# Clustered attention with token mixing: a twelve-slot plan for the two row halves of TensorE, small products in the maxima's PSUM tiles, and six weight conversions moved from the first half of the kernel to the second

## The chip, the cores and the metric

One core of one Trainium2 chip runs the whole kernel. The metric is device time in microseconds (us). Engines are named as in the profile: PE (TensorE matmul), PEld (its weight loads), DVE (VectorE), ACT (ScalarE), POOL (GpSimd), and SP, which issues nearly all DMAs; all but PEld take their instructions strictly in the order of their queue.

## The reference

```python
# attention: q, k, v are (4, 8, 768, 64), centroids (8, 16, 64)
q_assign = argmax(einsum('bhsd,hcd->bhsc', q_n, c_n)); k_assign likewise      # normalised rows
scores = where(q_assign[..., :, None] == k_assign[..., None, :], q @ k.T / sqrt(64), -1e9)
attn = exp(scores - max(scores)); attn = attn / (sum(attn) + 1e-9); x = attn @ v
# token mixing: x is (4, 768, 512)
theta = x @ w_theta
y = w_tok_r @ (x * cos(theta)) + w_tok_i @ (x * sin(theta))
u = x + y
return u + maximum(u @ w_ch, 0)
```

The weights arrive as 64-bit floats and are turned into 32-bit ones on the chip: one chunk is a DMA, an Abs on ACT, four integer and clamp operations on DVE (`to_f32`), a copy on ACT (the high part) and a subtraction on POOL (the low part).

## The kernel before

**Attention.** Two heads form a pair; there are 16 pairs. A pair has two halves `a` of 384 queries, and a half has six units, one for each block of 128 keys: 12 units a pair, 192 in all, numbered `u`. The main loop does two units in a pass, so a pair takes six passes. They are called pass 0, 2, 4, 6, 8 and 10 here, by `u` modulo 12.

In the PE the two heads of a pair use different halves of the 128 rows (`j` = 0: rows 0 to 63, `j` = 1: rows 64 to 127), so that two matmuls run beside each other; such a place in time is a *slot*. A pass has:

- the scores of two units, `sc`: four matmuls for each unit and head (`hk·hq`, `hk·lq`, `lk·hq`, and the mask and shift rows `mk·mq`), 8 slots; each unit and head fills one PSUM bank, of which there are three, and ACT reads it as an exponential into `at` (`exps`);
- the running maximum of a unit that is `LEAD` = 10 ahead, `m`: four matmuls for each head, 4 slots; each head fills one *maximum's tile* of two banks (tag `m`, two buffers), which DVE reduces to `nm` (`max_of`, the instruction at L396);
- the weighted sums `av` of the two units before (`weighted`): eight instructions of 32-bit floats;
- POOL adds the exponentials (`add_exps`), DVE adds two of those sums at `ADDS` (`acc` from `acc` and `acc`, L452).

**The small pieces.** `todo` holds pieces of work with a unit number at which they are issued (`at_unit`, `stages`); `pieces(x)` issues all up to x. For the pair after the next, `assign` finds the clusters: `lg` (centroid products, PE), `lt` (its transpose, PE; DVE then takes the maximum `mxl`, the equality and its product with the cluster numbers `eq`, and the maximum `rr`), `rt` (PE), a DMA round trip into `clq` and `clk`, and the mask rows `mq` and `mk`. `shift_row` transposes the row maxima (`mt`), `sums` adds over keys (`sm`, then a DMA round trip with a reciprocal on DVE), `normalise` scales `xt` on POOL. In the kernel before, `lg`, `mt`, `sm` use one of the three score banks, `lt` a maximum's tile, and all follow the weighted sums. After them, a pass ends with a further group of four slots.

Within attention `in_order` fixes the order of every engine as the code writes it. Instructions of the token mixing are ordered by the scheduler.

**The conversions.** `early_weights` converts 16 chunks during attention, one every 12 units: `w_theta` (4), the first three row blocks of `w_tok_r` and `w_tok_i` (6), and the last three of each (6), which are written back to DRAM in 32 bits (`w_d`). In the mixing, `late` loads these six (`kept`), splits them with one ACT copy and one DVE subtraction each, and converts `w_ch` (4 chunks).

**Token mixing.** 24 steps (4 batches × 6 blocks `t`): `theta` two steps ahead of `mix`; after six steps `channel` adds y and multiplies by `w_ch`. Step (0, t) of the first batch needs `w_r[t]` and `w_i[t]`.

Of the kernel before, what the change touches and what calls it, by code (L numbers as in the profile page):

```python
# [9 lines left out]
F32 = mybir.dt.float32  # L10
# [15 lines left out]
SUMS = (4, 6, 8, 9, 10)  # L26
# [3 lines left out]
EARLY = 3  # L30
NAT = 6
# [10 lines left out]
def kernel(  # L42
# [62 lines left out]
    ncl = cpool.tile([P, 1], F32, name="ncl")  # L105
    nc.vector.tensor_scalar_mul(ncl, mcl, -1.0)
# [43 lines left out]
    def split_w(hi, lo, src, cols, new, eng, most, kept=None):  # L150

        def chunk(sl):
            w = yield from to_f32(src[:, sl], sl.stop - sl.start, new)
            yield
            if kept is not None:
                nc.sync.dma_start(out=kept[:, sl], in_=w)
                return
            nc.scalar.copy(out=hi[:, sl], in_=w)
            eng.tensor_tensor(out=lo[:, sl], in0=w, in1=hi[:, sl].bitcast(F32), op=ALU.subtract)
# [15 lines left out]
    w_d = {(t, x): dram.tile([P, S], F32, name=f"wd{t}{x}") for t in range(EARLY, NT) for x in "ri"}  # L175
# [6 lines left out]
    ps = actx.enter_context(tc.tile_pool(name="ps", bufs=8 - 2 * N_M - N_AV, space=PSUM))  # L182
# [16 lines left out]
    def bank(name):  # L199
        return ps.tile([P, 512], F32, tag="bank", name=name)  # L200
# [47 lines left out]
    def assign(pi):  # L248
# [11 lines left out]
        lg = bank(f"lg{pi}")[:, 0:HS]  # L260
# [11 lines left out]
        for t in range(HS // P):  # L272
# [8 lines left out]
            out=eq, in0=ltv, in1=mx.unsqueeze(2).broadcast_to([P, NG, C]), op=ALU.is_equal)  # L281
        yield

        nc.vector.tensor_tensor(out=eq, in0=eq, in1=wb, op=ALU.mult)
# [29 lines left out]
        else:  # L314
            rt = bank(f"rt{pi}")[0:NG, 0:P]
# [23 lines left out]
        nc.vector.tensor_scalar(  # L339
            out=st[pi]["mk"], in0=cl["k"], scalar1=mcl, scalar2=mbi, op0=ALU.not_equal, op1=ALU.mult)  # L340
# [59 lines left out]
    def shift_row(pi, a):  # L400

        s = st[pi]
        mt = bank(f"mt{pi}{a}")
# [17 lines left out]
    def score_products(u, j, banks=None):  # L421
# [5 lines left out]
        sc = banks[:, j] if banks else ps.tile([P, 512], F32, tag="bank", name=f"sc{u}_{j}")  # L427
# [4 lines left out]

    def exps(u, j):

        pi, a, i = split_u(u)
        s = st[pi]
        last_exp[0] = nc.scalar.activation(out=s["at", a, i][:, j], in_=s["sc", j], func=AF.Exp, scale=SCALE)  # L437

    def add_exps(u):
# [6 lines left out]
        if y > 0:  # L446
            prev = s["at", a, i - 1] if y == 1 else s["acc", a, x]
            last_acc[0] = nc.gpsimd.tensor_tensor(out=s["acc", a, x], in0=prev, in1=at, op=ALU.add)  # L448

# [85 lines left out]
    def early_weights():  # L535
# [5 lines left out]
        for t in range(EARLY, NT):  # L541
            for x, src in (("r", wrT), ("i", wiT)):
                yield from split_w(
                    None, None, src[t * P:(t + 1) * P], S, raw_pair, nc.gpsimd, CKE, kept=w_d[t, x])
# [107 lines left out]
    A_UNITS = (-9, -4, -2, -1, 2, 2, 3, 6, 7, 7.9)  # L652
# [8 lines left out]
    A_THIRD = (-9, -1, 0, 1, 4, 4, 5, 7, 8, 9)  # L661
    W_EVERY = 12
# [17 lines left out]
    part_lo(0, "k", nc.gpsimd)  # L680
    load_v(0)
    in_order(start)
    for pi in range(NPAIR):
# [4 lines left out]
        for a in range(2):  # L688
            at_unit(u + a * NT - LEAD + NT, shift_row, pi, a)
# [317 lines left out]
```

## Time and profile before

| what | value |
|---|---|
| time, median of 3 runs | 791.12 us (791.0 to 792.93) |
| the profiled execution: its time, its span | 792.87 us, 791.1 us |
| mean granted PE clock | 0.991 |
| attention (up to the last `sm`) | to about 455.7 us |
| PE busy, DVE busy, POOL busy, ACT busy | 98%, 72%, 62%, 49% of the span |
| DMA | 73.43 MB |

The first half of the profile's 40 slices shows PE, DVE and POOL at 8 or 9 tenths at once, the second half only PE. A busy PE in this profile says that some matmul is recorded as running, not that they follow each other as closely as they can; gaps between the starts of matmuls are read from the timeline.

### The profile page before, as it was taken

To read this page: it belongs to the slowest core of one execution; us is meant where nothing else is said; L and a number is where in the kernel's file an instruction comes from. 1 tells how busy PE (TensorE), PEld (TensorE's weight loads), DVE (VectorE), ACT (ScalarE), POOL (GpSimd) and SP (SyncE) were. 2 spreads that over 40 slices of the span, in tenths; PEclk is the share of its full clock that TensorE was granted. 3 is DMA by queue.
4 is the path that set the end of the run, shared out by engine and by line. 5 is a ranking of instruction groups with operands and counts; after the bars stand their busy time and mean duration, and the time that the engine had idled before them with its cause. 6 is when DMAs were issued, how large, how long until landed. Compare 5 with 4: busy or idle time off the path is not lost.

```text
span 791.1 us, 14306 instructions
## 1 busy us (share of the span) xinstructions
PE 774.3 (98%) x5538; PEld 572.9 (72%) x5538; DVE 572.6 (72%) x688; ACT 386.5 (49%) x777; POOL 488.3 (62%) x284
## 2 busy tenths in 40 slices
PE   6999999999999999999999799999999999999998
PEld 4656665666656565656665488899889988899998
DVE  5789999999999999999989659954445433634322
ACT  3366666767676676767556436341334123403310
POOL 3388789999999999888988432561215122332131
PEclk9899999999999999999999999999999999999999
DMA  3132324332433244324343467115011411030001
GB/s 120 61 98 72 93 95 151 93 123 91 151 104 125 81 149 151 119 84 164 112 161 109 101 182 206 24 31 173 15 27 28 160 27 27 14 94 15 1 21 61
DMA packets 81583, 73.43 MB, mean 93 GB/s; under 512 B 59588, under 2 KB 65324, under 8 KB 81132
## 3 DMA queue, kind: packets, MB, share of 16 engines
q1 hardware_dynamic: 81228, 72.10, 30.5%
q8 instruction: 43, 0.70, 0.4%
q10 hardware_dynamic: 288, 0.43, 0.1%
q14 instruction: 24, 0.20, 0.1%
HBM read 57.08 MB, written 15.32 MB: 92 GB/s over the span
## 4 chain that ended last, share of the span: by engine, by line
PE 91%; DVE 5%; DMA 2%; issue 1%; SPq 1%; ACT 1%; DVEq 0%
PE y L876 26%; PE sc L374 24%; PE av L509 15%; PE tp L608 8%; PE cy L899 5%; PE m L374 4%; PE cp L899 3%; PE sm L476 2%; PE lg L263 2%; PE y L899 1%; DVE acc L452 1%; PE lt L275 1%; DVE nm L396 1%; PE mt L404 1%; DVE xl L583 1%
## 5 line engine op out<-in xcount | busy, mean ns | idle before, releaser
L437 ACT ACTIVATE at<-sc 128x384 f32<-128x384 f32 x384 | 173.6, 493 | 96.0 <-PE m L374 50.5
L396 DVE TENSOR_REDUCE nm<-m 128x1 f32<-128x768 f32 x192 | 179.6, 945 | 21.4 <-PE m L374 18.3
L448 POOL TENSOR_TENSOR acc<-at,at 128x768 f32<-128x768 f32 x64 | 129.9, 2030 | 36.0 <-ACT at L437 36.0
L374 PE MATMUL m<-hk,hq 64*128 64x384 f32 x384 | 147.1, 387 | 0.9 <-DVE nm L396 0.8
L509 PE MATMUL av<-at,vt 128*64 128x384 f32 x768 | 145.7, 499 | 1.4 <-ACT at L437 1.2
L830 POOL TENSOR_TENSOR zlc<-ab,zhc 128x512 fp32r<-128x512 f32 x24 | 32.1, 1336 | 173.2 <-ACT zhc L828 173.2
L448 POOL TENSOR_TENSOR acc<-acc,at 128x768 f32<-128x768 f32 x64 | 132.4, 2068 | 10.1 <-ACT at L437 8.0
L374 PE MATMUL m<-mk,mq 64*128 64x384 f32 x384 | 127.7, 336 | 0.8 <-DVE mk L303 0.8
L374 PE MATMUL sc<-hq,hk 64*128 64x384 f32 x384 | 116.6, 388 | 0.5 <-ACT at L437 0.5
L374 PEld LDWEIGHTS sc<-hq,hk 64*128 64x128 f32 x384 | 55.8, 184 | 62.7 <-issue 27.9
L374 PE MATMUL sc<-mq,mk 64*128 64x384 f32 x384 | 97.6, 335 | 0.0
L374 PE MATMUL sc<-hq,lk 64*128 64x384 f32 x384 | 97.3, 334 | 0.0
L374 PE MATMUL sc<-lq,hk 64*128 64x384 f32 x384 | 97.3, 334 | 0.0
L509 PEld LDWEIGHTS av<-at,vt 128*64 128x64 f32 x768 | 46.7, 136 | 60.5 <-issue 53.6
L374 PEld LDWEIGHTS m<-hk,hq 64*128 64x128 f32 x384 | 70.7, 185 | 3.4 <-DVE nm L396 2.8
L374 PEld LDWEIGHTS m<-mk,mq 64*128 64x128 f32 x384 | 71.6, 188 | 1.1 <-ACT hq L356 1.1
L613 DVE TENSOR_SCALAR kk<-tp 128x512 int32<-128x512 f32 x24 | 16.4, 683 | 77.2 <-PE tp L608 77.2
L452 DVE TENSOR_TENSOR acc<-acc,acc 128x768 f32<-128x768 f32 x30 | 70.6, 2354 | 0.0
L581 ACT CAST xh<-xT 128x512 fp32r<-128x512 f32 x23 | 14.3, 622 | 99.7 <-PE tp L608 99.7
L890 POOL TENSOR_TENSOR ul<-xT,uh 128x384 fp32r<-128x384 f32 (+1 forms) x36 | 33.5, 957 | 35.4 <-ACT uh L889 34.9
L374 PEld LDWEIGHTS sc<-lq,hk 64*128 64x128 f32 x384 | 54.9, 186 | 0.0
L374 PEld LDWEIGHTS sc<-mq,mk 64*128 64x128 f32 x384 | 54.7, 184 | 0.0
(160 smaller groups left out, 1710.3 us busy)
## 6 DMA issues: line engine op xcount, KB each, us to landing
rawq<-in_qT_dram SPq DMA_DIRECT2D x16, 384.0 KB
vt<-in_v_dram SPq DMA_DIRECT2D x16, 384.0 KB
rb<-sd SPq DMA_DIRECT2D x32, 192.0 KB
xT_d<-xt SPq DMA_DIRECT2D x16, 384.0 KB
xb<-xT_d SPq DMA_DIRECT2D x96, 64.0 KB
rawk<-in_kT_dram SPq DMA_DIRECT2D x15, 384.0 KB
w<-in_wrT_dram SPq DMA_DIRECT2D x6, 768.0 KB
w<-in_wiT_dram SPq DMA_DIRECT2D x6, 768.0 KB
```

The source lines that it names most:

```text
L374: nc.tensor.matmul(out, lhsT=stat[r, cols], rhs=mov[r, over], start=start, stop=stop)
L396: nc.vector.tensor_reduce(out=s["nm", a][:, j, i // 2:i // 2 + 1], in_=s["m", j][:, :, 0:HS], op=ALU.max, axis=AX.XY, negate=True)
L437: last_exp[0] = nc.scalar.activation(out=s["at", a, i][:, j], in_=s["sc", j], func=AF.Exp, scale=SCALE)
L448: last_acc[0] = nc.gpsimd.tensor_tensor(out=s["acc", a, x], in0=prev, in1=at, op=ALU.add)
L452: nc.vector.tensor_tensor(out=s["acc", a, 0], in0=s["acc", a, 0], in1=s["acc", a, 1], op=ALU.add)
L509: nc.tensor.matmul(s["av"][64 * j:64 * j + 64], lhsT=s["vt"][:, i, j, :], rhs=s["at", a, i][:, j], start=(i == 0), stop=(i == NT - 1))
L608: nc.tensor.matmul(tp, lhsT=xx[:, c, :], rhs=w_th[c][k], start=(n == 0), stop=(n == 3 * NCT - 1))
L613: nc.vector.tensor_scalar_mul(kk, tp, INV_2PI)
L830: nc.gpsimd.tensor_tensor(out=zl, in0=tr, in1=zh.bitcast(F32), op=ALU.subtract)
L876: nc.tensor.matmul(y_at(b, d, c0, c1), lhsT=zz[:, d * P:(d + 1) * P], rhs=ww[:, c0:c1], start=first and lead, stop=last, skip_group_check= ...
L890: nc.gpsimd.tensor_tensor(out=ul[:, d, :], in0=x, in1=uh[:, d, :].bitcast(F32), op=ALU.subtract)
L899: nc.tensor.matmul(cp, lhsT=w_c[d][k][:, e * P:(e + 1) * P], rhs=uu[:, d, :], start=(n == 0), stop=(n == 3 * NCT - 1), skip_group_check=True)
```

## The change

1. **A pass in twelve slots.** While maxima are still to be made, `two_units(u, v)` replaces the three groups. Each row half has its own list: rows `j` = 0 hold the last slot of the scores (u-1, 0), then m(v, 0) in slots 1 to 4, sc(u, 0) in 5 to 8, and the first three slots of sc(u+1, 0) in 9 to 11, whose fourth is carried into the next pass; rows `j` = 1 hold sc(u, 1) in 0 to 3, m(v, 1) in 4 to 7, sc(u+1, 1) in 8 to 11. The exponentials follow after slots 0, 3, 8 and 11, `max_of` after 4 and 7. The pieces of `pieces(u - 0.5)` and the weighted sums come after slot 11.
2. **Banks by a plan.** `bank` picks the score bank that a count of slots (`free_at`) says is free first.
3. **Small pieces.** `lg`, `rt`, `mt` and `sm` now take a maximum's tile, and by their new unit numbers (`SUMS`, `A_UNITS`, `shift_row` half a unit earlier) all stand in front of the weighted sums, after the twelve slots.
4. **Masks.** `mk` is made by one ACT pass (Abs with a scale and bias for each partition), `mq` by one DVE pass; before, `mq` took two ACT passes and `mk` one on DVE. The constants are made by `mask_constants`. The equality of `lt` is written in place in PSUM, and its product with the cluster numbers reads it from there.
5. **Conversions.** The six chunks that went through DRAM are no longer converted in attention. The remaining nine after the first start at units 0, 12, 36, 48, 72, 84, 108, 120, 144. `late` converts the six from the 64-bit input as 12 chunks of 384 columns, `LATE` says after which.
6. An explicit wait of `exps(u, 0)` on the adds and exponentials of unit u-5.

```diff
-SUMS = (4, 6, 8, 9, 10)
+SUMS = (3.5, 6, 8, 9, 10)
+LATE = (1, 3, 6, 8)
...
+    def bank(name, until=None):
+        x = min(range(NB), key=lambda i: (free_at[i], i))
+        free_at[x] = until if until is not None else clock[0] + AV_SLOTS
+        return ps.tile([P, 512], F32, tag=f"bank{x}", name=name)
...
-        lg = bank(f"lg{pi}")[:, 0:HS]
+        lg = (m_tile(f"lg{pi}")[:, 0] if pi > 2 else bank(f"lg{pi}"))[:, 0:HS]
...
         nc.vector.tensor_tensor(
-            out=eq, in0=ltv, in1=mx.unsqueeze(2).broadcast_to([P, NG, C]), op=ALU.is_equal)
-        yield
-
-        nc.vector.tensor_tensor(out=eq, in0=eq, in1=wb, op=ALU.mult)
+            out=ltv, in0=ltv, in1=mx.unsqueeze(2).broadcast_to([P, NG, C]), op=ALU.is_equal)
+        nc.vector.tensor_tensor(out=eq, in0=ltv, in1=wb, op=ALU.mult)
+        yield
...
-            nc.scalar.activation(out=mq, in_=cl["q"], func=AF.Abs, bias=ncl)
-            yield
-            nc.scalar.activation(out=mq, in_=mq, func=AF.Relu, scale=-1.0, bias=1.0)
+        nc.scalar.activation(out=st[pi]["mk"], in_=cl["k"], func=AF.Abs, scale=kscale, bias=kbias)
         yield
         nc.vector.tensor_scalar(
-            out=st[pi]["mk"], in0=cl["k"], scalar1=mcl, scalar2=mbi, op0=ALU.not_equal, op1=ALU.mult)
+            out=st[pi]["mq"], in0=cl["q"], scalar1=mcl, scalar2=-1.0, op0=ALU.is_equal, op1=ALU.mult)
...
-        mt = bank(f"mt{pi}{a}")
+        mt = m_tile(f"mt{pi}{a}")[:, 0] if pi + a > 0 else bank(f"mt{pi}{a}")
...
+        v = u + 1 - NAT
+        for x in (adds[v], exp_of[v, 0], exp_of[v, 1]) if j == 0 and v in adds else ():
+            tc.add_manual_dep(last_exp[0].ins, x.ins.name, ...)
...
+        begin = {
+            0: (scores, u, 1, 0, 4), 1: (maxima, 0, 1), 4: (maxima, 1, 4), 5: (scores, u, 0, 5, 9),
+            8: (scores, u + 1, 1, 8, 12), 9: (scores, u + 1, 0, 9, SLOTS + AV_SLOTS + 1)}
+        end = {
+            0: first, 3: [(exps, u, 1), (weighted_out, u - 3)], 4: [(max_of, v, 0)], 7: [(max_of, v, 1)],
+            8: [(exps, u, 0), (add_exps, u)], 11: [(exps, u + 1, 1)]}
+        for k in range(SLOTS):
+            ...
+            interleave(*([rows[j, k]] for j in range(2) if (j, k) in rows))
+            for fn, *a in end.get(k, ()):
+                fn(*a)
...
-        sm = bank(f"sm{pi}") if pi < NPAIR - 1 else ...
+        sm = m_tile(f"sm{pi}")[:, 0] if pi < NPAIR - 1 else ...
...
-    A_UNITS = (-9, -4, -2, -1, 2, 2, 3, 6, 7, 7.9)
+    A_UNITS = (-9, -2.5, -0.5, 0, 1.5, 2, 3, 7, 7.9)
-    W_EVERY = 12
...
-            at_unit(u + a * NT - LEAD + NT, shift_row, pi, a)
+            at_unit(u + a * NT - LEAD + NT - (0.5 if pi + a > 0 else 0), shift_row, pi, a)
...
-        stages(W_FIRST if x == 0 else [W_EVERY * (x - 1) + k for k in W_UNITS], gen)
+        stages(W_FIRST if x == 0 else [NU * (3 * (x - 1) // 2) + k for k in W_UNITS], gen)
...
-        if 0 <= u < NUT:
+        if 0 <= u and ahead < NUT:
+            two_units(u, ahead)
+        elif 0 <= u < NUT:
+            finish(u - 1)
             both(score_products, u, exps)
...
     def late():
-        for t in range(EARLY, NT):
-            for w, x in ((w_r, "r"), (w_i, "i")):
-                hi, lo = w[t]
-                kept = u_tile("kept").rearrange("p c s -> p (c s)").bitcast(F32)[:, 0:S]
-                nc.sync.dma_start(out=kept, in_=w_d[t, x])
-                nc.scalar.copy(out=hi, in_=kept)
-                nc.vector.tensor_tensor(out=lo, in0=kept, in1=f(hi), op=ALU.subtract)
...
+        rows = [(w[t], src, S, t) for t in range(EARLY, NT) for w, src in ((w_r, wrT), (w_i, wiT))]
+        rows += [(w_c[c], w_ch, DM, c) for c in range(NCT)]
+        for x, (hi_lo_, src, cols, r) in enumerate(rows):
+            for gen in split_w(*hi_lo_, src[r * P:(r + 1) * P], cols, wt_pair, nc.gpsimd, CK):
+                run(gen)
+            if x in LATE:
+                yield
```

**Two places in the order of the engines.** Names carry the unit (`m156_0`: unit 156, head 0; the number behind it counts tiles). Unit 144 is pass 0 of pair 12, unit 146 pass 2; the maxima made there are those of units 154 and 156.

DVE from pass 0 to pass 2, before:

```order
L396 TENSOR_REDUCE nm150_4569<-m152_1_4638 128x1
L278 TENSOR_REDUCE mxl14_4660<-lt14_4656 128x24
L280 TENSOR_TENSOR eq14_4662<-lt14_4656,mxl14_4660 128x384
L396 TENSOR_REDUCE nm150_4569<-m152_0_4665 128x1
L284 TENSOR_TENSOR eq14_4662<-eq14_4662,wc_74 128x384
L286 TENSOR_REDUCE rr14_4678<-eq14_4662 128x24
L396 TENSOR_REDUCE nm150_4569<-m154_1_4695 128x1
L396 TENSOR_REDUCE nm150_4569<-m154_0_4713 128x1
L452 TENSOR_TENSOR acc139_4547<-acc139_4547,acc142_4634 128x768
L396 TENSOR_REDUCE nm156_4745<-m156_1_4746 128x1
L137 TENSOR_SCALAR w32_4605<-w32_4605 128x768
L396 TENSOR_REDUCE nm156_4745<-m156_0_4777 128x1
```

DVE at the same place, now:

```order
L403 TENSOR_REDUCE nm150_4516<-m154_0_4631 128x1
L403 TENSOR_REDUCE nm150_4516<-m154_1_4639 128x1
L291 TENSOR_REDUCE mxl14_4668<-lt14_4664 128x24
L293 TENSOR_TENSOR lt14_4664<-lt14_4664,mxl14_4668 128x384
L295 TENSOR_TENSOR eq14_4670<-lt14_4664,wc_74 128x384
L299 TENSOR_REDUCE rr14_4678<-eq14_4670 128x24
L471 TENSOR_TENSOR acc139_4514<-acc139_4514,acc142_4601 128x768
L403 TENSOR_REDUCE nm156_4689<-m156_0_4690 128x1
L403 TENSOR_REDUCE nm156_4689<-m156_1_4699 128x1
```

The four steps behind `lt` and the add of `acc` now stand in one run between the second maximum of pass 0 and the first of pass 2; before, a maximum stood between them at two places.

PE at the end of pass 2's slots, before (`m156_1` is the maximum's tile filled last; `mt121` holds the transposes of the row maxima and of `rr`):

```order
L374 MATMUL sc147_0_4744<-mq_0_165,mk_0_166 128x384
L374 MATMUL m156_1_4746<-mk_1_148,mq_1_147 128x384
L509 MATMUL av144_4758<-at144_4680,vt12_4550 64x384 x2
L509 MATMUL av144_4758<-at145_4693,vt12_4550 64x384 x2
L404 MATMUL mt121_4763<-identf_64,nm150_4569 6x128
L312 MATMUL mt121_4763<-identf_64,rr14_4678 24x128
L374 MATMUL sc147_1_4776<-hq_0_161,hk_0_163 128x384
L374 MATMUL m156_0_4777<-hk_1_145,hq_1_143 128x384
```

PE at the same place, now:

```order
L381 MATMUL sc147_0_4717<-hq_0_155,lk_0_158 128x384
L381 MATMUL sc147_1_4712<-mq_0_159,mk_0_160 128x384
L411 MATMUL mt121_4725<-identf_64,nm150_4516 6x128
L325 MATMUL mt121_4725<-identf_64,rr14_4678 24x128
L567 MATMUL av144_4735<-at144_4625,vt12_4506 64x384 x2
L567 MATMUL av144_4735<-at145_4651,vt12_4506 64x384 x2
L381 MATMUL sc147_0_4717<-mq_0_159,mk_0_160 128x384
L381 MATMUL sc148_1_4752<-hq_0_155,hk_0_157 128x384
```

`mt121` now stands in front of the weighted sums, and the tile it takes is the buffer that `m156_0` held in the same pass, two tiles earlier; in the built program it waits for DVE's reduction of `m156_0`. `lg` in pass 10, `lt` in pass 0, `sm` in pass 4 and the other `mt` in pass 8 stand in the same way; pass 6 has no small piece.

More of the change, by code (lines that the diff above doesn't have):

```diff
@@ L148, in to_f32, with split_w @@
         return w
-    def split_w(hi, lo, src, cols, new, eng, most, kept=None):
+    def split_w(hi, lo, src, cols, new, eng, most):
         def chunk(sl):
@@ L426, in score_products @@
             s["at", a, i] = p3.tile([P, 2, HS], F32, tag="at", name=f"at{u}", bufs=NAT)
-        sc = banks[:, j] if banks else ps.tile([P, 512], F32, tag="bank", name=f"sc{u}_{j}")
+        sc = banks[:, j] if banks else bank(f"sc{u}_{j}", until)
         sc = s["sc", j] = sc[:, 0:HS]
@@ L437, in exps @@
         last_exp[0] = nc.scalar.activation(out=s["at", a, i][:, j], in_=s["sc", j], func=AF.Exp, scale=SCALE)
+        exp_of[u, j] = last_exp[0]
+        v = u + 1 - NAT
+        for x in (adds[v], exp_of[v, 0], exp_of[v, 1]) if j == 0 and v in adds else ():
+            tc.add_manual_dep(
+                last_exp[0].ins, x.ins.name,
+                mybir.DependencyInfo(mybir.DependencyClass.Sync, mybir.DependencyReason.DATA),
+                reason="use of the tile that the next unit's exponentials write")
     def add_exps(u):
@@ L448, in add_exps @@
             last_acc[0] = nc.gpsimd.tensor_tensor(out=s["acc", a, x], in0=prev, in1=at, op=ALU.add)
+            for v in (u - 1, u) if y == 1 else (u,):
+                adds[v] = last_acc[0]
     def add_sums(pi, a):
```

95 lines of the change are left out of this document (55 added, 40 removed).

## The prediction

> **What bounds the kernel now.** I read the page first, then the busy time of the engines over six equal pairs of the attention, then the chain that ended last, then the timeline of single passes, and last the groups of DVE.
>
> ```profile
> span 791.1 us, 14306 instructions
> PE 774.3 (98%) x5538; PEld 572.9 (72%) x5538; DVE 572.6 (72%) x688; ACT 386.5 (49%) x777; POOL 488.3 (62%) x284
> ```
>
> ```profile
> 178.40:334.10 155.70, 155.70 (x1288) 94.82 (x1286) 147.64 (x145) 104.71 (x222) 150.48 (x72) 1.00 0.38 117
> ```
>
> The columns of the second fence are the window, its length, then busy PE, PEld, DVE, ACT, POOL, the granted clock, DMA share and GB/s. These are six pairs of 25.95 us: PE always busy, DVE 95%, POOL 97%, ACT 67%. So three engines are nearly full, and the chain decides between them:
>
> ```profile
> 197.09 1.44 PE av L509 x8
> 198.53 0.78 PE sm L476 x8
> ...
> 207.10 0.20 PE mt L404
> 207.30 0.78 PE lg L263 x8
> ...
> 211.97 0.48 PE lt L275 x3
> ...
> 220.49 0.11 PE mt L312
> ...
> 223.04 1.44 PE av L509 x8
> ```
>
> The chain stays on PE through the pair (from one av at 197.09 to the same av at 223.04: 25.95). The timeline of one pass shows how close PE's starts are:
>
> ```profile
> 203.15 0.44 PE L374 MATMUL sc<-hq,hk 64*128 64x384 f32 x1
> 203.43 0.33 PE L374 MATMUL sc<-lq,hk 64*128 64x384 f32 x1
> ...
> 204.15 0.49 ACT L437 ACTIVATE at<-sc 128x384 f32<-128x384 f32 x1 [0.96 <-PE m L374]
> ...
> 204.48 0.34 PE L374 MATMUL sc<-mq,mk 64*128 64x384 f32 x2
> ...
> 204.69 0.44 PE L374 MATMUL sc<-hq,hk 64*128 64x384 f32 x1
> 204.97 0.33 PE L374 MATMUL sc<-lq,hk 64*128 64x384 f32 x1
> ...
> 205.32 0.34 PE L374 MATMUL sc<-mq,mk 64*128 64x384 f32 x1
> 205.59 0.87 PE L509 MATMUL av<-at,vt 128*64 128x384 f32 x4
> 205.72 0.96 DVE L396 TENSOR_REDUCE nm<-m 128x1 f32<-128x768 f32 x1 [0.58 <-PE m L374]
> ```
>
> Slots start 0.17 us apart (six of them from 203.43 to 204.48). The first slot after the weighted sums takes 0.28, the last in front of them 0.27. In between, the group at 204.69 starts when the exponential of 204.15 has ended (204.64): its bank was the last of three. That costs 0.04 of waiting and 0.11 of a slower first slot, 0.15 a pass, 0.9 a pair. Everything else on PE is work: 6 × (0.28 + 11 × 0.17 + 0.10 + 1.44) = 22.1 and pieces of 0.78 + 0.78 + 0.48 + 0.11 + 2 × 0.20 = 2.55; with the 0.9, 25.6 of 25.95. So PE can win about 0.9 a pair from a better order, no more, and DVE and POOL must then follow in 25.05.
>
> ```profile
> L396 DVE TENSOR_REDUCE nm<-m 128x1 f32<-128x768 f32 x73 | 68.3, 944 | 5.9 <-PE m L374 5.3
> L452 DVE TENSOR_TENSOR acc<-acc,acc 128x768 f32<-128x768 f32 x12 | 29.3, 2445 | 0.0
> L143 DVE SCALAR_TENSOR_TENSOR w<-w,w 128x768 int32<-128x768 int32 x6 | 10.3, 1716 | 0.0
> L284 DVE TENSOR_TENSOR eq<-eq,wc 128x384 bf16<-128x384 bf16 x6 | 8.6, 1432 | 0.0
> L137 DVE TENSOR_SCALAR w<-w 128x768 f32<-128x768 f32 x6 | 8.0, 1329 | 0.0
> L339 DVE TENSOR_SCALAR mk<-clk,mcl,mbi 128x768 fp32r<-128x768 f32 x6 | 7.4, 1228 | 0.0
> L280 DVE TENSOR_TENSOR eq<-lt,mxl 128x384 bf16<-128x384 f32 x6 | 3.3, 557 | 0.2
> ```
>
> ```profile
> 243.87 1.83 POOL L448 TENSOR_TENSOR acc<-at,at 128x768 f32<-128x768 f32 x1 [0.42 <-ACT at L437]
> 244.21 2.30 DVE L452 TENSOR_TENSOR acc<-acc,acc 128x768 f32<-128x768 f32 x1
> 412.81 0.95 DVE L452 TENSOR_TENSOR acc<-acc,acc 128x768 f32<-128x768 f32 x1
> 412.83 2.61 POOL L448 TENSOR_TENSOR acc<-acc,at 128x768 f32<-128x768 f32 x1
> ```
>
> The last four rows matter most. DVE's add of two SBUF tiles takes 0.95 when it starts just ahead of a POOL add (which then takes 2.61 instead of 1.83), and 2.30 when POOL's add started first: it ends 0.81 after POOL's end at 245.70. One waits for the other; the mean over six pairs is 2.445. The equality that reads PSUM takes 0.557, its product from SBUF 1.432: reading PSUM spares the wait, so the product in its new form is taken at 0.56.
>
> **The change part by part.**
>
> *Twelve slots, banks.* The tightest bank is that of sc(u+1, 0): needed at slot 9 (0.28 + 8 × 0.17 = 1.64 after the pass's start), free after the exponential behind slot 3, at 0.62 + 0.33 + 0.05 + 0.49 = 1.5. So the 0.15 goes in most passes: -0.9 a pair. ACT pieces at the end of a pass can push it back by a few tenths; one ACT pass of the masks less makes that smaller.
>
> *Small pieces in a maximum's tile.* There are two such buffers, and a pass now asks for three: m(v, 0), m(v, 1), piece. So the piece needs the buffer of m(v, 0) of the same pass, and PE, in order, holds the weighted sums behind it. The piece is queued ahead of both weighted sums and the whole next pass. When DVE is prompt it fits: slot 4 starts at 0.79, its result reaches DVE at 1.2 (as 205.32 to 205.72), the first maximum ends at 2.1, the second at 3.0; the piece is due at 0.28 + 11 × 0.17 + 0.10 = 2.25. The margin is 0.1, and any DVE work still queued from the pass before lands on PE. Two places have such work.
>
> Pass 0 to 2. Pass 0 lasts 2.25 + 0.48 (lt) + 1.44 = 4.2. DVE after the second maximum at 3.0 does mxl, eq, product and rr (four of 0.56, each waiting for the last), until about 5.2, then `acc`. If alone (0.95), `acc` ends at 6.1; at its mean (2.445) at 7.6. The first maximum of pass 2 could start at 4.2 + 1.2 = 5.4; it ends at 7.0 or 8.5. The transposes are due at 4.2 + 2.25 = 6.45: PE waits 0.6 or 2.1. Which one: POOL's add of the next exponential is released by pass 2's slot 0, at 4.2 + 0.44 + 0.49 + 0.1 = 5.2, the same tenth. Either may be first, so I take the middle, 1.3. The Trainium skill (SBUF — State Buffer, "SBUF: two separate sides") gives the shared ports to whichever of the two engines' instructions starts first, to its end; by that rule there is no middle: `acc` ends at 6.1, or behind the whole POOL add at 5.2 + 1.83 + 0.95 = 8.0, and a wait of 0.6 or 2.5 would make the 1.3 × 13 = 17 of the sum 8 or 32. The pairs of rows at 244 and 412 agree with the rule; which engine comes first here no run shows.
>
> Pass 8 to 10. Pass 8 lasts 3.73 + 0.20 = 3.9. After 3.0 DVE has `mq` (as L339, 1.23), `acc` (2.445) and a short reciprocal (some 0.2, an estimate from the 0.56 of 384 columns): until 6.9, or 4.8 if neither waits for POOL (0.6 by half of L339, and 0.95). The first maximum of pass 10 is ready at 5.1; it ends at 7.85 or 6.0; `lg` is due at 6.15: PE waits 1.7 or nothing. POOL has two adds queued at that time, then a gap of a few us, so one of the two DVE steps waits and the other not: 1.0.
>
> *Conversions in attention.* Nine chunks instead of fourteen over pairs 1 to 13 (0.69 a pair). Two DVE steps of 1.33 stand in pass 2, behind maxima that are already late: 0 to 0.5 on pass 4's `sm`, 0.15 a pair on average. The chunks that are gone took about 5 us of DVE each (L137 twice at 1.33, L143 at 1.72, one more), beside PE's work: no gain of their own while PE sets the end. POOL's eleven operations of 1.83 to 2.6 a pair remain, about 24 of 25: cover for a PE that is slower, a second limit for one that is faster.
>
> *Masks, waits, constants.* ACT does one pass less (it is 67% busy), DVE the same. The wait on the adds of unit u-5 is for work issued two passes earlier, 8 us, against a POOL backlog of one operation (2.6): 0. The eight constants at the start lie beside the first maxima's matmuls: 0.
>
> So a pair: -0.9 + 1.3 + 1.0 + 0.15 = +1.55, over the 13 pairs that have `lt`, `mq` and `lg`: +20.
>
> *End of attention.* The last conversion stood on the chain there:
>
> ```profile
> 434.33 2.52 DVE w L146
> ...
> 437.28 2.06 DMA sq<-sd
> ...
> 439.59 0.56 DVE kk L613
> ```
>
> Without it the reciprocal's round trip starts 2.5 us earlier, and next the exponentials and the step at 445 set the pace: -2 (0 to -4).
>
> *Late conversions.*
>
> ```profile
> 462.00:475.00 13.00, 13.00 (x75) 11.32 (x74) 6.82 (x12) 3.10 (x5) 3.33 (x3) 1.00 0.56 161
> 475.00:519.00 44.00, 44.00 (x238) 37.83 (x237) 39.34 (x52) 23.27 (x38) 17.87 (x12) 1.00 0.39 104
> L137 DVE TENSOR_SCALAR wtmp<-wtmp x4: 414/416/1526, 490.1 to 498.7; 128x512 f32<-128x512 f32 x4
> L143 DVE SCALAR_TENSOR_TENSOR wtmp<-wtmp x4: 679/686/1779, 491.0 to 503.8; 128x512 int32<-128x512 int32 x4
> ```
>
> Twelve chunks of 384 columns, four DVE steps each, two as L137 and two as L143, scaled by 0.75: 1.65 a chunk alone, 5 beside POOL; 20 us in all if alone. Six subtractions of 768 columns go to POOL (0.95 each if alone): net +14 for DVE, which has 4.7 + 6.2 idle until 519. So some 3 us too much, which the final sums wait for: +3 (0 to +15, if POOL, then busier than its 40%, holds half the steps). DMA has room (share 0.39); the SP queue loses the six stores and has twelve loads for six.
>
> Sum: +20 - 2 + 3 = +21 on the profiled execution's 792.87 (span 791.1 and 1.8 around it), so 813.9; the median shown lies 1.75 lower: 812.
>
> **The rivals.**
>
> *PE runs free, faster.* DVE is first at the shared ports and prompt at both places: waits of 0.6 and 0 become small against what the order gains elsewhere. For it: DVE's load falls, by L284's 0.9 and a third of the conversions, and 412.81 shows the short form. Against it: the short form is one row, the other twelve average 2.445. With no wait at all -0.9 × 13 - 2 = -14: 777; with the short waits -0.3 × 13 - 2 = 785. It decides where `acc` in pass 0 starts before POOL's add.
>
> *Both waits at their full price, and the late stage.* -0.9 + 2.1 + 1.7 + 0.15 = +3.05 a pair, +40 over 13, and -2 + 3: 832 and up. For it stand the twelve long adds; against it the gap in POOL's work before each place.
>
> *The late conversions alone decide.* Attention comes out even (waits near 1 a pair cancel the 0.9) and the late stage costs 0 to 10: 789 to 800. For it: DVE's 39.34 of 44 busy; against it: none of the waits there are PE's before.
>
> *A lower clock after each wait.*
>
> ```profile
> 452.00:456.00 4.00, 3.12 (x17) 1.09 (x18) 4.00 (x6) 0.77 (x3) 1.73 (x1) 0.50 0.93 292
> 452.88 2.79 PE L476 MATMUL sm<-acc,ecol 128*32 128x384 f32 x16 [2.46 <-DVE xt L522]
> ```
>
> After 2.46 idle the granted clock stood at 0.50 for 4 us. If a wait of 2.1 did that, each would cost 2 us more: 13 × 2 = +26, some 838. Against it: that gap followed another, the waits here stand between dense slots. The Trainium skill (TensorE: Matmul & The Clock Gate, "Why this matters for your kernels") warns only of gaps beyond some 3 us; by that rule there is none here.
>
> **How the numbers follow.** Waits in the middle of their bounds (800 to 828): 0.49. Full waits or a lower clock (above 828): 0.12. Even attention (789 to 800): 0.13. Free PE (below 789): 0.26. The likeliest gives 812. The range leaves out about a tenth at each end, 779 to 838; the likeliest case's own is 800 to 828. Within 0.3% (2.4 us, about what a measurement of this kernel tells from no change) lie 788.7 to 793.5. So faster 0.26, same 0.05, slower 0.69.
>
> **What would show it.** In attention: idle time of PEld before `mt` and `lg`, released by the maximum's reduction, 1 to 2 us in passes 2 and 10, none before `sm`; a pair of 27 to 28 us; no more wait for the exponential in the middle of a pass. `acc` at 2.4 right before those waits. DVE and POOL below 95%. PE gaps in the first batch of the mixing, at `channel`, of a few us. Wrong would be: a pair at or under 25.5 with `acc` at 1 us in pass 0, or PE waits at other tiles (banks, ACT).

## The result, and the profile after

The changed kernel takes 833.77 us (median of 4 runs, 831.71 to 838.43), the kernel before 792.02 beside it (791.0 to 793.49): 1.0534 times as long, 95% interval 1.0484 to 1.0583. The forecast was 812. The profiled execution took 834.54. The page of the changed kernel begins:

```profile
span 832.7 us, 14372 instructions
PE 771.4 (93%) x5538; PEld 576.9 (69%) x5538; DVE 531.0 (64%) x713; ACT 394.6 (47%) x776; POOL 488.3 (59%) x295
PEclk8799999999999999999999989978999999999999
```

PE's busy time has hardly moved (774.3 to 771.4), while the span grew by 41.6: PE waits now. Where, the starts of five instructions tell, read from the groups of each tile:

| stretch | before | after | difference | forecast |
|---|---|---|---|---|
| start to first `mt` | 27.1 | 30.6 | +3.5 | 0 |
| to the first `mt<-identf,rr` | 36.3 | 39.5 | +3.2 | +1.55 (the 13th pair) |
| 12 pairs, to the last `mt<-identf,rr` | 312.7 | 330.3 | +17.6 | 12 × 1.55 = +18.6 |
| to the first `y` (end of attention) | 86.1 | 87.3 | +1.2 | -2 |
| to the first `cp` (first batch) | 61.7 | 72.5 | +10.8 | +3, with the row below |
| to the end | 267.2 | 272.5 | +5.3 | |

The pairs came out as forecast, 27.52 us for 26.06. The waits of PE in six of them (columns: engine, tile and line, releaser, then us in all, times, longest):

```profile
PE lg L276 <- DVE nm L403: 6.4, 6, 1.2
PE mt L411 <- DVE nm L403: 5.9, 9, 1.5
PE sm L534 <- DVE nm L403: 0.7, 4, 0.2
```

That is 13.0 of the 14.2 us in which PE is not busy there; the sixth wait of pass 2, 1.44 before 345.6, is cut by the window's end and makes up the rest. Before, the same view of six pairs has no row at all. The window itself, to be put beside the one of before (155.70 long, DVE 147.64, POOL 150.48):

```profile
180.20:345.30 165.10, 150.89 (x1282) 94.51 (x1278) 127.02 (x136) 104.73 (x212) 142.67 (x71) 1.00 0.33 100
```

Two passes of the timeline show each wait with what stood in front of it. Pass 2, twice (DVE's add, POOL's neighbours, then PE):

```profile
287.69 0.95 DVE L471 TENSOR_TENSOR acc<-acc,acc 128x768 f32<-128x768 f32 x1
287.79 2.52 POOL L465 TENSOR_TENSOR acc<-at,at 128x768 f32<-128x768 f32 x1 [0.54 <-ACT at L447]
289.56 0.27 PE L411 MATMUL mt<-identf,nm 128*6 128x128 f32 x1 [0.50 <-DVE nm L403]
...
258.65 1.85 POOL L590 TENSOR_TENSOR xt<-xt,rb 128x768 f32<-128x768 f32 x1 [1.19 <-DMA rb<-sd]
259.68 1.64 DVE L471 TENSOR_TENSOR acc<-acc,acc 128x768 f32<-128x768 f32 x1
260.45 2.53 POOL L465 TENSOR_TENSOR acc<-at,at 128x768 f32<-128x768 f32 x1
262.24 0.27 PE L411 MATMUL mt<-identf,nm 128*6 128x128 f32 x1 [1.19 <-DVE nm L403]
```

Where `acc` starts ahead of POOL it takes 0.95 and PE waits 0.50; where a POOL product (`xt`, 258.65 to 260.50) is running it takes 1.64, and PE waits 1.19. Pass 10:

```profile
220.41 2.59 DVE L471 TENSOR_TENSOR acc<-acc,acc 128x768 f32<-128x768 f32 x1
223.36 0.23 DVE L552 RECIPROCAL sq<-sq 128x12 f32<-128x12 f32 x1 [0.35 <-DMA sq<-sd]
223.50 1.75 DVE L403 TENSOR_REDUCE nm<-m 128x1 f32<-128x768 f32 x2
224.45 0.51 PE L276 MATMUL lg<-rawq,cb 128*32 128x384 f32 x1 [1.18 <-DVE nm L403]
```

The maximum that frees the tile for `lg` begins only when `acc` and the reciprocal are over, and the reciprocal itself waited 0.35 for a DMA.

The second loss is in the first mixing batch. Three windows of it come first, and one from the kernel before (columns as in the prediction: length, PE, PEld, DVE, ACT, POOL, clock, DMA share, GB/s):

```profile
545.00:561.00 16.00, 5.48 (x29) 4.62 (x28) 16.00 (x23) 7.25 (x13) 11.31 (x7) 0.73 0.20 47
560.20:569.60 9.40, 9.01 (x24) 7.36 (x25) 6.33 (x14) 5.90 (x12) 8.38 (x8) 0.51 0.15 24
569.60:583.00 13.40, 13.40 (x78) 13.26 (x77) 4.24 (x8) 0.00 (x0) 3.21 (x4) 1.00 0.27 92
...
523.90:528.10 4.20, 4.20 (x25) 4.17 (x24) 1.88 (x5) 2.51 (x6) 4.20 (x5) 1.00 0.33 51
```

Then the longest wait of PE there:

```profile
PE cp L948 <- ACT uh L938: 10.5, 1, 10.5
```

And the timeline ahead of its end:

```profile
553.42 1.75 DVE L152 SCALAR_TENSOR_TENSOR wtmp<-wtmp 128x512 int32<-128x512 int32 x1
...
556.77 1.75 DVE L155 SCALAR_TENSOR_TENSOR wtmp<-wtmp 128x512 int32<-128x512 int32 x1
...
559.03 0.74 DVE L936 TENSOR_TENSOR xT<-y,xT 128x384 f32<-128x384 f32 x2
559.67 0.51 ACT L938 CAST uh<-xT 128x384 fp32r<-128x384 f32 x1 [0.50 <-DVE xT L936]
```

DVE is busy for all of the 16 us of the first window, in which PE stands for 10.5; the final sums (L936) come behind the last conversion steps, so ACT's copy, which the wait names, is not the cause. From the first `y` to these sums DVE did 17.3 us more than before (the first two windows are from now, the last from before):

```profile
487.70:516.00 28.30, 28.30 (x159) 24.52 (x158) 20.48 (x35) 10.24 (x20) 11.23 (x9) 1.00 0.58 155
516.00:559.00 43.00, 33.71 (x181) 28.55 (x179) 43.00 (x65) 20.51 (x39) 24.67 (x17) 0.92 0.43 112
...
462.20:519.00 56.80, 56.80 (x310) 48.96 (x309) 46.16 (x63) 26.37 (x43) 21.00 (x15) 1.00 0.43 117
```

Its idle time fell only from 10.6 to 7.8 us, and all of the 7.8 lies ahead of 516. So the sums come 14.5 us later after the first `y`; PE had other work for 4.0 of that and waited 10.5.

After the gap the clock stands at 0.51 for 9.4 us. The 24 matmuls issued in that time took 4.2 us before, at a clock of 1.00: that is 5.2 of the 5.3 us in the last row of the table.

### The profile page after: what moved, and what is told of

Read it like the earlier page. It is cut to its first block, busy times and chain, and to the rows that moved or that the text cites. A ratio compares the mean times of both kernels' runs of the same rounds, so it can differ in the third digit from the quotient of the medians.

```text
span 832.7 us, 14372 instructions
## 1 busy us (share of the span) xinstructions
PE 771.4 (93%) x5538; PEld 576.9 (69%) x5538; DVE 531.0 (64%) x713; ACT 394.6 (47%) x776; POOL 488.3 (59%) x295
## 4 chain that ended last, share of the span: by engine, by line
PE 61%; DVE 28%; DMA 5%; issue 2%; ACT 2%; SPq 1%; POOL 1%; DVEq 0%; ACTq 0%
PE y L925 18%; PE av L567 11%; DVE nm L403 9%; PE sc L381 8%; PE tp L664 6%; PE m L381 5%; PE cy L948 5%; DVE acc L471 3%; PE cp L948 3%; DVE w L155 2%; DMA sq<-sd 2%; PE lg L276 2%; DVE w L149 2%; PE sm L534 1%; DVE wtmp L155 1%
## 5 line engine op out<-in xcount | busy, mean ns | idle before, releaser
L447 ACT ACTIVATE at<-sc 128x384 f32<-128x384 f32 x384 | 185.3, 491 | 126.3 <-PE sc L381 122.5
L381 PE MATMUL sc<-mq,mk 64*128 64x384 f32 x384 | 135.4, 360 | 0.0
L381 PE MATMUL m<-hk,hq 64*128 64x384 f32 x384 | 116.0, 346 | 2.7 <-DVE nm L403 1.9
L381 PE MATMUL m<-mk,mq 64*128 64x384 f32 x384 | 115.0, 342 | 0.7 <-DVE kbias L111 0.7
L381 PE MATMUL sc<-lq,hk 64*128 64x384 f32 x384 | 111.0, 336 | 0.0
L381 PE MATMUL sc<-hq,lk 64*128 64x384 f32 x384 | 110.5, 335 | 0.0
L381 PEld LDWEIGHTS sc<-mq,mk 64*128 64x128 f32 x384 | 69.6, 185 | 53.5 <-issue 53.4
L381 PEld LDWEIGHTS sc<-hq,hk 64*128 64x128 f32 x384 | 68.9, 184 | 9.7 <-ACT at L447 2.5
L381 PEld LDWEIGHTS sc<-hq,lk 64*128 64x128 f32 x384 | 68.3, 185 | 0.0
L471 DVE TENSOR_TENSOR acc<-acc,acc 128x768 f32<-128x768 f32 x30 | 57.2, 1908 | 0.9 <-POOL acc L465 0.9
```

The source lines that it names most:

```text
L381: nc.tensor.matmul(out, lhsT=stat[r, cols], rhs=mov[r, over], start=start, stop=stop)
L471: nc.vector.tensor_tensor(out=s["acc", a, 0], in0=s["acc", a, 0], in1=s["acc", a, 1], op=ALU.add)
```

## The experiments

Each ratio is to runs of the kernel before on the same chip, whose medians were 792.3, 792.5, 793.3 and 792.3. Line numbers shift a little where lines were added.

**1. Only the conversions moved, in the kernel before.**

```diff
-                yield from split_w(
-                    None, None, src[t * P:(t + 1) * P], S, raw_pair, nc.gpsimd, CKE, kept=w_d[t, x])
...
-        stages(W_FIRST if x == 0 else [W_EVERY * (x - 1) + k for k in W_UNITS], gen)
+        stages(W_FIRST if x == 0 else [NU * (3 * (x - 1) // 2) + k for k in W_UNITS], gen)
...
-                nc.sync.dma_start(out=kept, in_=w_d[t, x])
...
+            for gen in split_w(*hi_lo_, src[r * P:(r + 1) * P], cols, wt_pair, nc.gpsimd, CK):
```

> The kernel before with only the conversions of part 5 moved (nine chunks instead of fourteen after the first in attention, twelve of 384 columns in the mixing). Theory A, DVE is the limit of the first mixing batch: that batch goes from 78.5 to about 95 us (the +16 seen between the two profiles), the end of attention gains 0 to 2, the total is 792 + 14 to 16 = 806 to 808. Theory B, the prediction's term (+3) was right and the other 13 us came from what the new attention leaves behind: 792 + 1 to 3 = 793 to 795.

806.9 us, ratio 1.0189 (1.0155 to 1.0224), +14.6. The pair stays at 26.06, the first `y` at 461.7 (462.2 before): nine chunks for fourteen are worth 0.5 us to the old attention. The batch has the same stop, and theory A holds:

```profile
519.00:535.00 16.00, 5.68 (x29) 4.51 (x28) 16.00 (x23) 7.47 (x14) 10.06 (x7) 0.72 0.17 40
PE cp L885 <- ACT uh L875: 10.3, 1, 10.3
```

**2. The same, without DVE's steps in those six conversions.**

```diff
         nc.scalar.activation(out=w, in_=high.bitcast(F32), func=AF.Abs)
+        if short:
+            return w
```

> The kernel before with only the conversions of part 5 moved, and in the six converted in the mixing DVE's four steps left out (the three last row blocks of both token weights then hold only the Abs of the high words; loads, ACT and POOL work stay). Theory A, DVE's load makes the first batch longer: DVE has 27 us less there, the batch falls back to 79 us, total 790 to 793. Theory B, the chain of twelve loads through four u tiles and POOL's subtractions makes it longer: total 803 or more.

798.3 us, 1.0069 (1.0046 to 1.0092). The wait at `cp` falls from 10.3 in one to 1.3 in two, the stretch from the first `y` to the first `cp` from 72.2 to 62.8. So DVE's steps make 8.6 of the 14.6 us. The other 5.8 are less than theory B wants and more than A: its profiled execution, the fastest of its runs (794.82), shows only 1.9 of them. In it the mixing is 4.0 us longer than before, 1.1 up to the first `cp`, which waits 0.9, and 2.9 behind it, where PE waits 1.6, both for the copies `uh`; attention is 2.1 shorter, with the same pairs. Whether the loads or POOL's subtractions, which were left in, make the copies late, no run shows.

**3. The conversions put back, in the changed kernel.**

```diff
+                yield from split_w(
+                    None, None, src[t * P:(t + 1) * P], S, raw_pair, nc.gpsimd, CKE, kept=w_d[t, x])
...
-        stages(W_FIRST if x == 0 else [NU * (3 * (x - 1) // 2) + k for k in W_UNITS], gen)
+        stages(W_FIRST if x == 0 else [NU * (x - 1) + k for k in W_UNITS], gen)
...
+                nc.sync.dma_start(out=kept, in_=w_d[t, x])
```

> The changed kernel with the conversions as before (fourteen chunks after the first in attention, one every 12 units, six through DRAM). Theory A: the first mixing batch falls back to about 79 us, the pairs stay at 27.5 or gain 0 to 0.3 us each from five more chunks; total 833.8 - 16 + 0 to 4 = 818 to 822. Theory B (the attention causes the loss in the first batch): stays at 830 or more.

830.91 us, 1.0500 (1.0446 to 1.0553). The first batch is back at 61.7 and `cp` waits 0.4; but the pair goes to 28.49. Attention gives back 11.6 of the 16. So both theories missed: the batch followed A, the pairs did not. The profiled execution is the slowest of its four (835.86), and 9.0 of the 11.6 us stand in three of its pairs, of 30.42, 31.97 and 29.78; the other nine take 27.74 on average, 0.2 more than in the changed kernel. In each of the three `lg` waits for 1.85 to 2.78 us. In two of them it does so behind a reciprocal that waits 1.85 and 0.94 for its load `sq`, which stands in SP's queue behind the store of a converted chunk too (`wd3r`), and whose data come 3.1 us after its issue in the first of them, for 1.8 in the changed kernel (221.60 to 223.36):

```profile
338.40 0.36 SPq L165 DMA_DIRECT2D wd3r<-w  x1
338.85 0.37 SPq L554 DMA_DIRECT2D sq<-sd  x1
341.92 0.23 DVE L556 RECIPROCAL sq<-sq 128x12 f32<-128x12 f32 x1 [1.85 <-DMA sq<-sd]
343.01 0.85 PE L280 MATMUL lg<-rawq,cb 128*32 128x384 f32 x1 [2.78 <-DVE nm L407]
```

In the third, `mq` took 2.22 beside POOL, for 0.6 in the two others. That the store's traffic makes the load slow is not shown. After each of the three waits the clock stands at 0.50, for 3.4, 6.8 and 3.4 us; at 1.00 that work would take some 6.8 less (an estimate, half of 13.6).

**4. The adds `acc` taken from DVE, in the changed kernel.**

```diff
-        nx = NT // TERMS if pi == NPAIR - 1 else 1
+        nx = NT // TERMS
-                at_unit(7 if pi == a == 0 else u + ADDS[a], add_sums, pi, a)
```

> The changed kernel without DVE's adds acc<-acc,acc; PE sums both accumulators instead (sm has twice the matmuls, +0.78 us of PE a pair). Theory A, these adds stand in front of the maximum for which mt and lg wait (2.3 us a pair in the prediction): waits before mt in pass 2 and lg in pass 10 fall below 0.3 us, the pair goes from 27.5 to 25.05 + 0.78 + 0.3 = 26.1; total 833.8 - 13 x 1.4 = 816. Theory B, a piece has to wait for the first maximum's tile whatever DVE has queued: the waits stay, the pair grows by 0.78 to 28.3; total 844.

831.58 us, 1.0502 (1.0450 to 1.0553); the pair is 27.22. The waits of six pairs:

```profile
PE lg L276 <- DVE nm L403: 7.1, 6, 1.3
PE sm L534 <- DVE nm L403: 2.4, 4, 1.3
```

`mt` waits no more: its wait was the add's. `lg` waits as before, and the timeline says for what:

```profile
214.18 0.61 DVE L346 TENSOR_SCALAR mq<-clq,mcl 128x768 fp32r<-128x768 f32 x1
217.62 0.23 DVE L552 RECIPROCAL sq<-sq 128x12 f32<-128x12 f32 x1 [2.82 <-DMA sq<-sd]
217.76 1.75 DVE L403 TENSOR_REDUCE nm<-m 128x1 f32<-128x768 f32 x2
```

DVE stood idle for 2.82 us in front of the maximum: the reciprocal is next in its queue, and its data are not there. SP's queue shows why they are late:

```profile
214.33 1.48 SPq L424 DMA_DIRECT2D mq<-mr  x2
215.90 0.35 SPq L550 DMA_DIRECT2D sq<-sd  x1
```

The load `sq` stands behind the store of `mr`, which needs the `mt` of pass 8. In the kernel before it went first (205.29 and 207.75 there): the change took `mt` half a unit forward, past the load. So `lg` had two covers, and taking one away shows nothing.

**5 and 6. The load `sq` in front of that store: alone, and without the adds.**

```diff
-SUMS = (3.5, 6, 8, 9, 10)
+SUMS = (3.5, 6, 7, 9, 10)
```

> The changed kernel with one number changed: the third of SUMS from 8 to 7, so that in SP's queue the load sq<-sd stands in front of the store mq<-mr of pass 8, which waits for mt, and no longer behind it. Theory A, lg has two covers of about the same length, the adds acc and the reciprocal that waits for this load (without the adds the wait before lg stayed at 1.2 us): with only the load moved the wait before lg falls by 0.3 us at most, total 830 to 834. Theory B, the load alone holds lg: the wait goes, 833.8 - 13 x 1.07 = 820.

> The changed kernel without DVE's adds (PE sums both accumulators, +0.78 us of PE a pair) and with sq<-sd loaded in front of mq<-mr. Theory A, both covers of lg are gone: its wait of 7.1 us in six pairs falls below 1, the pair goes from 27.2 to 26.1; total 831.6 - 13 x 1.1 = 817. Theory B, lg waits for the maximum for another reason (conversions, masks): no change, 829 to 833.

Alone: 829.14 us, 1.0470 (1.0443 to 1.0498); `lg` waits 4.8 us in six pairs, for 6.4. Together: 824.13 us, 1.0401 (1.0360 to 1.0441), pair 26.43; `lg` is gone from the waits of PE, and what is left is `sm`, in the four pairs of six that have a chunk:

```profile
PE sm L534 <- DVE nm L403: 6.6, 4, 1.8
```

Two covers, as theory A had it. The total is 7 us above its number: the pair is 0.33 longer than it had it, with 1.1 a pair now waited at `sm` (0.4 before), which makes 4 us over 13; what the other 3 are is not shown.

**7. The adds moved, not removed.**

```diff
-SUMS = (3.5, 6, 8, 9, 10)
+SUMS = (3.5, 6, 7, 9, 10)
-ADDS = (8, 13)
+ADDS = (10, 14)
-    W_UNITS = (8, 11.5, 14, 15, 16, 18, 19.5)
+    W_UNITS = (8, 11.5, 16, 16, 16, 18, 19.5)
```

> The changed kernel with DVE's adds moved by two units and one (ADDS 10, 14, ends of pass 10 and pass 2), sq<-sd in front of mq<-mr, and the conversions' DVE steps three at the end of pass 4 and one at the end of pass 6, where no piece follows at once. DVE's work is the same. Theory A, it is the place of DVE's work in front of a piece and not its amount that costs: waits before mt and lg below 0.3 each, pair at 25.3 to 25.9; total 833.8 - 13 x 1.75 = 811. Theory B, DVE beside POOL has too much work in all: waits appear at other pieces (lt, sm, the first m), the pair stays above 27, total above 826.

831.77 us, 1.0519 (1.0470 to 1.0569), the total of theory B; the pairs of its profile (828.75 us) average 26.89, which neither theory has. But the waits in six pairs are four and four, all in pairs with a chunk:

```profile
PE mt L411 <- DVE nm L403: 7.0, 4, 1.8
PE m L381 <- DVE nm L403: 5.2, 4, 1.5
```

A pair without a chunk runs free (from one `mt<-identf,rr` to the next, 25.01):

```profile
203.62 0.27 PE L325 MATMUL mt<-identf,rr 128*24 128x128 f32 x1
...
228.63 0.27 PE L325 MATMUL mt<-identf,rr 128*24 128x128 f32 x1
```

So the adds, with the load `sq` in front, cost nothing in a pair without a chunk, and the conversion steps, which I had put together at the ends of passes 4 and 6, now cost some 3 us a chunk:

```profile
237.13 2.46 DVE L152 SCALAR_TENSOR_TENSOR w<-w,w 128x768 int32<-128x768 int32 x1
239.52 1.80 DVE L403 TENSOR_REDUCE nm<-m 128x1 f32<-128x768 f32 x2
241.25 2.63 DVE L155 SCALAR_TENSOR_TENSOR w<-w,w 128x768 int32<-128x768 int32 x1
243.81 1.81 DVE L403 TENSOR_REDUCE nm<-m 128x1 f32<-128x768 f32 x2
```

**8. No conversion steps on DVE in attention** (`return w` behind the Abs, as in 2, for the nine chunks).

> The changed kernel with DVE's four conversion steps left out of the nine chunks after the first in attention (those nine then hold only the Abs of the high words; loads, ACT and POOL work stay). Theory A, in the changed order a chunk costs some 0.5 us (0.33 before mt in pass 8 and 0.18 before sm, as the waits of the profile have it): nine chunks 5 us, the waits in passes 2 and 10 stay at 0.5 to 1.0, total 829. Theory B, a chunk costs 2.3 us (five more chunks made the pair 0.97 longer in the run with the old conversions): nine chunks 21 us, total 813.

833.28 us, 1.0501 (1.0460 to 1.0543), pair 27.47. DVE's load falls to 104.72 of 166.00 us, and the two waits stay:

```profile
183.00:349.00 166.00, 152.53 (x1290) 95.39 (x1286) 104.72 (x120) 104.61 (x213) 135.72 (x71) 0.99 0.32 100
PE lg L280 <- DVE nm L407: 7.4, 6, 1.5
PE mt L415 <- DVE nm L407: 6.0, 6, 1.6
```

In these places the amount of DVE's work does not count: with DVE 63% busy the pair is as long as with 77%. Theory B is out; A's 5 us didn't show either. The profile of the changed kernel agrees: its pairs with a chunk of 768 columns wait 0.51 at `sm` and at `mt` of pass 8, but only 0.83 on average at the `mt` of pass 2 that ends them, for 1.38 in the pairs without a chunk; so they are 0.15 longer (27.69 for 27.54). Five more chunks at this price do not make the 11.6 us of run 3, whose three long pairs have the causes named there.

**9. The pieces behind the weighted sums.**

```diff
-SUMS = (3.5, 6, 8, 9, 10)
+SUMS = (4, 6, 8, 9, 10)
-    A_UNITS = (-9, -2.5, -0.5, 0, 1.5, 2, 3, 7, 7.9)
+    A_UNITS = (-9, -2, 0, 0, 2, 2, 3, 7, 7.9)
-            at_unit(u + a * NT - LEAD + NT - (0.5 if pi + a > 0 else 0), shift_row, pi, a)
+            at_unit(u + a * NT - LEAD + NT, shift_row, pi, a)
```

> The changed kernel with lt, mt, rt, lg and sm behind the weighted sums instead of in front of them (still in a maximum's tile), the twelve slots kept. Theory A, the loss in the pairs is PE standing in front of 1.44 us of work that it could have done: the waits shrink by up to 1.44 each, the pair goes to 25.3 to 26.0; total 833.8 - 13 x 1.8 = 810. Theory B, DVE's lateness only moves to the maxima of the next pass (slots 1 and 4 need the tiles): the pair stays at 27 or above; total 827 or more.

833.9 us, 1.0539 (1.0499 to 1.0579), pair 27.37. The wait changes its place, as theory B said: the tile of `lt` is now read by DVE when the next pass asks for it.

```profile
PE m L381 <- DVE eq L295: 5.5, 6, 0.9
PE lg L276 <- DVE nm L403: 2.5, 4, 0.9
```

**10. The start.**

```diff
+    mask_constants()
     ecol = cpool.tile([P, 32], F32, name="ecol")
...
-        free_at[x] = until if until is not None else clock[0] + AV_SLOTS
+        free_at[x] = until if until is not None else clock[0] + AV_SLOTS + 0.01 * next(turn)
...
-    mask_constants()
     load_v(0)
```

> The changed kernel with the start mended in two places: the eight small DVE steps of mask_constants stand with the other constants, ahead of the first DMA's end, and the plan of the banks takes a different bank each time while its clock stands still (in the changed kernel the two ot tiles of pair 0 get the same bank, and PE waited 0.89 us for ACT to read the first). Theory A, these two are the start's loss: the first mt moves from 30.6 back to about 28 us (the 0.89, the 0.74 behind the constants, and some of the slower clock after them), total 831 to 832. Theory B, the first pairs' loss comes from the order of DVE's steps there: the first mt stays at 30 or above, 833 to 835.

831.05 us, 1.0470 (1.0441 to 1.0500): not to be told from the changed kernel. The wait of 0.89 is gone. The one of 0.74 was no loss: PE waits there for `mk`, 0.84 in the kernel before and 0.59 here, and the constants only ended last. The first `mt` still comes at 31.2: with the constants ahead, DVE took the 0.96 of `lq` before the reduction for `cs`, on which the first `lg` waits. One profile cannot settle the rest: in runs 3 to 8, with the start of the changed kernel, the first `mt` came between 28.2 and 30.9, and in runs 11 and 12, with the mended start, at 28.9 and 28.5.

**11 and 12. Everything together**, the conversions as in the kernel before:

```diff
-ADDS = (8, 13)
+ADDS = (8, 14)        # run 12: (7, 14)
-    W_UNITS = (8, 11.5, 14, 15, 16, 18, 19.5)
+    W_UNITS = (12, 15.5, 16, 17, 18, 22, 23)        # run 12: (..., 17, 20, 22, 23)
```

> Twelve slots with DVE's steps placed by what the runs showed: adds at the ends of passes 8 and 2, sq<-sd in front of mq<-mr, a chunk's DVE steps at the ends of passes 4 (two), 6 and 10, mt of the first half behind the weighted sums, the start mended, all sixteen conversions in attention as in the kernel before (six through DRAM). Theory A, place decides: PE waits 0.3 to 1.0 a pair (lg), the pair is 25.3 to 25.9, total 792 - 13 x 0.2 to 0.8 + 0 to 3 = 782 to 792. Theory B, DVE beside POOL is full (26.3 us of DVE work in a pair with a chunk, worked out from the means of the runs): the pair is 26.5 or more, total 798 or more.

> As the one before it, with the first half's adds at the end of pass 6, a chunk's third step at the end of pass 8, and lg behind the weighted sums too. Theory A: waits of lg go, those of the first m of a pass may come (0 to 0.5), pair 25.1 to 25.7, total 780 to 790. Theory B: 26.5 or more a pair, 798 or more.

807.61 us, 1.0179 (1.0145 to 1.0214), and 808.89, 1.0196 (1.0170 to 1.0222): 26 us better than the change, 15 worse than the kernel before. The pairs are 26.76 and 26.85, theory B's numbers. But its reason, a full DVE, is not seen: the first run has it at 136.56 of 160.60 us, and PE's recorded waits come to 1.2 a pair, spread over `lg`, `m` and `mt`. The size of a chunk does count here: in run 12 the three pairs with chunks of 512 columns take 25.57 to 25.76, the six with 768 columns and POOL's subtraction 27.23 to 27.78, the three with 768 columns and a store in its place 27.10, 26.45 and 25.46. Why is open.

```profile
173.70:334.30 160.60, 153.30 (x1268) 94.61 (x1266) 136.56 (x142) 104.56 (x211) 138.34 (x71) 1.00 0.38 115
```

No version tried beats the kernel before.

## Why the prediction was wrong where it was wrong

- **The slots, -0.9 a pair: right.** The free pair of run 7 is 25.01, against 25.95: -0.94. PE free of waits would take 25.05, the prediction said.
- **The wait in pass 2, +1.3 (0.6 to 2.1): right in place and cause.** Six of them in the changed kernel are 0.50, 0.89, 1.19, 0.50, 1.53 and 1.44: mean 1.0. Run 4 shows the adds behind it. They lie between the bounds, where the prediction had seen a choice of two ends, because POOL often runs another instruction there, the product `xt`, and is part done with it when `acc` comes: the 1.64 of `acc` at 259.68 is the 0.82 left of `xt` and 0.82 more. The Trainium skill (SBUF — State Buffer, "SBUF: two separate sides") lets the instruction that came first keep the shared ports to its end; the trace agrees with that, 0.95 ahead of POOL and 1.64 behind it.
- **The wait in pass 10, +1.0: right in size, half the cause.** 0.98 to 1.18, mean 1.06. The prediction named `mq`, `acc` and the reciprocal, and took the reciprocal at its own 0.2 us. It did not follow the SP queue, where `mt` passed the load `sq`: runs 4 to 6 show this second cover.
- **Conversion steps in attention, +0.15: the waits larger, the cost about right.** 0.18 before `sm` and 0.33 before the `mt` of pass 8 (a place that it had not named), in four of six pairs: 0.34 in waits. But a pair with a chunk is only 0.15 longer than one without, and run 8, without DVE's steps, is no faster. The four terms add up to -0.94 + 1.0 + 1.06 + 0.34 = 1.46, and the twelve pairs grew by 1.46 each. That the two agree to the hundredth is luck: the six pairs of the measured waits grew by 1.71 (27.66 for 25.95), and 0.25 of that is in none of the terms.
- **Late conversions, +3: the failed step, with +16 measured** (14.6 alone in run 1). Two parts of the term were wrong and one was missing. The price: twelve chunks were put at 20 us of DVE; the groups of `wtmp` on DVE between 487.6 and 561 sum to 38.9, of which the four of `w_ch` had 11.4 before: 27.5, so the net is 27.5 - 7.9 = 19.6, not 14. The idle time: the prediction let all of DVE's 4.7 + 6.2 take work in; only 2.8 of it did, since 7.8 us stayed idle ahead of 516, and behind 516 there was none left. Missing was the price after the stop, the clock: 5.2 us. The upper end of 15 covers the first two; I had chosen a value near the lower. That DVE's steps are the cause, run 2 shows for 8.6 of run 1's 14.6 us.
- **End of attention, -2: wrong in sign, +1.2.** Run 1 prices the step that is gone: with only the conversions moved, the row is 85.8, 0.3 less than before and not 2. PE's wait before `tp`, the product with `w_theta`, falls there from 1.40 to 0.52. Behind that, the chain of the changed kernel runs over ACT's exponentials and the DMA `rb<-sd`, as it did before. The row also holds some three pairs of attention, whose new order the prediction put at nothing; the other 1.5 us come with it, and where is not shown.
- **The start, 0: wrong, +3.5, and not by the constants.** A plan of banks whose clock stands still gives the same bank twice: 0.89 of waiting that the prediction did not look for. The product of `eq` takes 0.56 from PSUM where pair 0 had it in 0.36 from SBUF, with POOL idle: 0.2 more. Most of the rest can be the clock: from 13 to 63 us it is 0.83, before 0.93, which is worth 5 us at most (an estimate, 0.10 × 50) of the 6.7 lost up to the first `mt<-identf,rr`. Runs 3 to 8 have the same start and lose 1.1 to 3.8 up to the first `mt`, so the +3.5 of one profile is no firm price.

Of the rivals, "a lower clock after each wait" did not come true in the pairs, whose waits were 1.78 at most (1.00 from 60 to 470 us), but it did after the one of 10.5. The prediction set it aside with a bound of some 3 us, and that bound is too high here: in run 3 waits of 1.85, 2.44 and 2.78 were enough.

## What to carry to other kernels

When work is put in front of another engine's queue, ask what each engine has waiting at that point, and follow every queue that the moved step overtakes, the one that only issues DMAs too: here a load that fell behind one store held PE as long as an addition of 2 us did. A wait with two covers doesn't move when one is taken away, so take both before calling either innocent. An engine's slack over a stage is worth nothing if the work must be done by a fixed point in it: DVE still stood idle for 7.8 us early in the first batch, and the last steps stood in front of the final sums all the same.

## What the hardware showed that was not expected

PE stood from 549.7 to 560.2. The granted clock was 1.00 up to 552.3, 0.50 from there to 569.4, which is 9.2 us after PE had work again, and then 1.00:

```profile
552.30:569.40 17.10, 8.81 (x23) 7.16 (x24) 14.23 (x22) 7.65 (x15) 14.80 (x12) 0.50 0.18 28
```

Run 1 shows the same: after a wait of 10.3 the clock is 0.50 up to 539.8, 5.9 us after PE's restart.

Shorter waits did it too. In the traces of all runs, from 60 us on, every wait of PE of 2.16 us or more was followed by 0.50 for 3.4 us or longer: the 2.46 before the last `sm`, which every run has, 2.44 and 2.78 in run 3, 2.37 in run 6, 2.16 in run 12. Of the waits between 1.6 and 2.0 some were (1.85 in run 3, 1.93 in run 8, 1.78 in run 10) and others were not (1.92 in run 3, 1.93 in run 10, 1.78 in the changed kernel). In the pairs, none below 1.6 was. So in this kernel a wait of 2 us can cost more than its length, and those of 1 us did not.
